# Batch 1's first transform stage partly moved ahead of the main loop, and its frequency groups started at unit 13

## The chip, the cores and the metric

The kernel runs on one core of one Trainium2 chip. The metric is the time of one execution in microseconds of device time (us). The kernel before takes 1475.23 us in the median of three runs (1474.01 to 1475.56). The core has TensorE (PE; its weight loads are shown apart as PEld), VectorE (DVE), ScalarE (ACT), GpSimd (POOL) and SyncE (SP), which here only issues transfers. Each engine works through its own instructions in the order in which the program lists them.

## What is computed

Cut to what matters (the layers follow one another; `relu`, `soft` and the top-1 choice are written out in words):

```
X = rfft(x, axis=1)                       # x: 8 batches, 3072 positions, 256 channels
Y = (Xr w_r - Xi w_i + b_r) + i (Xr w_i + Xi w_r + b_i)
Y = soft(Y, 0.01)                         # real and imaginary part apart
y = irfft(Y, n=3072)                      # 24576 tokens of 256 channels
g = s * relu(y w_in)**2 + b ; z = g w_out # 256 -> 2048 -> 256
e = argmax(z w_gate)                      # one of 8 experts per token
out = gate * (relu(z w1[e]) w2[e])        # for the first 768 tokens of each expert, else 0
```

## The kernel before, in words

**The transform.** A sequence of 3072 is taken as 48 times 64. The first stage (`f1_mm`, L223) multiplies by a 48-point table: one call takes 8 of the 64 residues of one batch, so a batch has 8 calls. A call reads an x tile of 384 KB that `f1_load` (L210) brought in by two transfers, makes four products (matmul, L235; two instructions each in fp32, so 8 in the trace), copies the result out of PSUM (for every batch but 0 with one ACT copy of 128x1024, L239, into a ring `z` of two buffers) and stores it to DRAM with two transfers (L248), for later batches by way of a list `later` that is emptied by `flush` after the next unit. The second stage works on 12 pairs of frequency groups per batch: `g_load` (L255) reads one pair from DRAM across all 64 residues, so it needs the stores of all 8 calls; `g_a` transforms (L269) and copies the result to `l` (ACT L272, DVE L273); `g_b` and `g_b2` multiply by the channel matrices (L346) and add the biases; `g_soft` thresholds; `g_c` is the inverse transform of the pair (L384) and stores it to `vd`. The last stage, `i2_do` (L485), loads eight tiles per batch from `vd` (`i2_load`, L397), multiplies (64 small products, L416), copies (ACT L419) and transposes on DVE (L431).

**The main loop.** What follows the transform is done in units, 64 per batch. `s_unit` (L755) makes 256 of the 2048 hidden columns for 384 tokens (four products, L764), a relu on ACT (L769) and a square on DVE (L770) into a ring `q` of nine buffers (`QB`). Eight units together give cheap logits (L784). All other work is hung on units by hand: `put(at, f, rank)` says before or after which unit a piece is emitted, and within a unit pieces go by rank, then by `at`. A planner `best(lo, hi, work)` chooses the unit of a few pieces by the load noted so far. Since every engine works in program order, this table is the schedule.

**Before the main loop** batch 0 is transformed alone: eight first-stage calls, 36 idle products (`warm`, L440: a product with a tile of zeros, written to a PSUM bank that nothing reads), then `first_groups` (L467), a list of 30 steps in which pairs 0 to 11 of batch 0 go by, with the conversion of the weights `moe_w_in` (blocks `CONV_A`) hung on eleven of these steps. A block's raw words are fetched (`conv_load`, L537), two ACT instructions make its low part and a square (`conv_low`, L559), six DVE instructions join the words (`conv_word`, L571), and `conv_use` splits the result. The fp32 results of `CONV_A` use the same nine buffers `q` as the squares later do, and so does the bias tile `bias0` (L188) for batch 0.

**The second conversion.** The blocks `CONV_B` (eight, of `moe_w_out`) have their raw words in the ring `x` of four buffers that also holds the x tiles of the first stage. One step n of `conv_items` (L623) fetches block n+3, makes the low part and the words of block n+2, transposes block n-1 (L606, ACT copy L608) and makes the gate products of block n-2 (L619). Blocks 0 to 3 are fetched in steps 16 to 22 of `first_groups`; three steps (`CONV_EARLY`) run ahead of `i2_do(0, 0)`, the other nine in units 0 to 6 (`MOE_CONV_AT`). So blocks 4 to 7 are fetched in units 0 to 3. In units 0 to 10 there are also the 32 pieces of `gram_items` (L656; products L665 and L677), and in units 7 to 11 `load_bias` and `bound_items` (L690), which end with the bound weights `wogb` that the first logits, in unit 13, need.

**Batch 1 and 2 in the units of batch 0.** The first-stage calls of batch 1 stand at units 6, 8, ... 20, those of batch 2 from unit 27. Each call of batch 1 also loads the x tile three calls ahead (`x_ahead`, L461); the first three are loaded in unit 4. The pairs of batch 1 begin at unit 26 (`FIRST_GROUPS_AT`) and follow each other every two units; `g_load` runs one to three units ahead of `g_a`. `load_bias1` and `sum_mix`, which `g_b` needs, stand at unit 15. Between `first_groups` and `i2_do(0, 0)` stand 11 idle products.

Of the kernel before, what the change touches and what calls it, by code (L numbers as in the profile page):

```python
# [130 lines left out]
INV_LOAD_AT = 55  # L131
FIRST_GROUPS_AT = 26
GROUP_LEAD = 10
# [13 lines left out]
WARM_F1 = 36  # L147
WARM_GROUPS = 11
MOE_CONV_AT = (0, 1, 2, 3, 3, 4, 5, 6, 6, 7, 7)
# [6 lines left out]
class Kern:  # L156
# [29 lines left out]
    def load_bias0(self):  # L186
        nc, I = self.nc, self.I
        b = self.stage()[:, 0:2 * C]  # L188
        for gi in range(2):
            for k in range(2):  # L190
                src = I[("b_r", "b_i")[(gi + k) % 2]].rearrange("(o c) -> o c", o=1)
                nc.sync.dma_start(out=b[64 * k:64 * k + 64, gi * C:(gi + 1) * C], in_=src.to_broadcast([64, C]))
        self.bias0 = b
# [16 lines left out]
    def f1_load(self, b, c):  # L210

        if b == 0 and c > 3:
            xp = (self.mo.tile([128, 4, C], F32, tag="u", name="x", bufs=3) if c < 7 else
                  self.wk.tile([128, 4, C], F32, tag="z", name="x", bufs=2))
        else:
            xp = self.wk.tile([128, 4, C], F32, tag="x", name="x", bufs=4)
# [6 lines left out]
    def f1_mm(self, b, c):  # L223

        nc = self.nc
        xp = self.xt.pop((b, c))
        if b or c % 2 == 1:
            ph = self.hp.tile([128, 2, 512], F32, tag="h", name="pz")
            ps = [ph[:, 0], ph[:, 1]]
        else:  # L230
            ps = [self.psum("pz") for r in range(2)]
        for k in range(2):
            for r in range(2):
                h = slice(64 * r, 64 * r + M1)
                nc.tensor.matmul(ps[r][64 * k:64 * k + 64, :], self.f1[h], xp[h, 2 * k:2 * k + 2].rearrange("p a c -> p (a c)"),  # L235
                                 start=True, stop=True, skip_group_check=True)
        if b:
            zz = self.wk.tile([128, 4, C], F32, tag="z", name="z", bufs=2)
# [208 lines left out]
    def f1_items(self, b):  # L447
        it = []
        for k in range(8):
            def f(k=k):  # L450
                self.f1_mm(b, k)
                if b:
                    self.x_ahead(8 * b + k + (XP if b < 3 else XP - 1))
            it.append(f)
# [104 lines left out]
    def conv_low(self, k):  # L559
# [3 lines left out]
        raw = self.cv[k]  # L563
        if raw.dtype == F32:
            return
# [1248 lines left out]
    def run(self):  # L1814
# [6 lines left out]
        with ExitStack() as es, tc.manual_schedule():  # L1821
# [54 lines left out]
            for n, k in enumerate((16, 18, 20, 22)):  # L1876
                extra[k] = lambda n=n: self.conv_load(CONV_B[n])
            for k, f in enumerate(gr):
                f()
# [4 lines left out]
                if not conv:  # L1884
                    conv = self.conv_items(CONV_B, 3, 2)
            self.warm(WARM_GROUPS)
            self.i2_load(0, 0)
            self.i2_load(0, 1)
            for k in range(CONV_EARLY):
                conv.pop(0)()  # L1890
            self.i2_do(0, 0)

# [52 lines left out]
            def groups(b):  # L1945
                at, cyc, steps = 64 * (b - 1) - GROUP_LEAD, GROUP_CYCLE, GROUP_STEPS
                if b == 1:
                    at, cyc, steps = FIRST_GROUPS_AT, 2, FIRST_STEPS
                elif b == B - 1:
# [19 lines left out]
            def plan_batch(b):  # L1969
                u = 64 * b  # L1970
                if b == 0:
# [10 lines left out]
                    put(52, lambda: self.route_consts(pp))  # L1982
                    put(15, lambda: (self.load_bias1(), self.sum_mix()))
                    put(54, lambda: (clear(self.list), clear(self.gd)))
                    put(4, lambda: self.x_ahead(7 + XP), 0)
                if b == B - 2:
# [28 lines left out]
                if b == 0:  # L2015
                    for k in range(8):
                        put(6 + 2 * k, self.f1_items(1)[k], 4)
                        put(27 + int(2.9 * k), self.f1_items(2)[k], 4)
                elif b + 2 < B:
# [93 lines left out]
```

## Time and profile before

| | |
|---|---|
| median of 3 runs | 1475.23 us (1474.01 to 1475.56) |
| the profiled execution's own time | 1474.91 us |
| its span, first to last instruction | 1473.1 us |
| PE busy | 1373.8 us, 93% of the span |
| DVE, ACT, POOL busy | 63%, 57%, 7% |
| mean granted clock of TensorE | 0.98 |

An engine's busy time says how long its instructions ran, not whether they ran at full speed: the granted clock of TensorE, a share of its full 2.4 GHz, stands beside it. A matmul row's count is of instructions, and `ph` or `pz` in a row is the tile written. In a timeline the bracket at the end of a row is the idle time of that engine just before it and the instruction that ended it. SPq is SP's queue of transfers. Time zero is the span's start.

### The profile page before, as it was taken

How to read it: one execution, taken by the hardware profiler on the slowest of the kernel's cores; microseconds unless marked ns; L12 is line 12 of the kernel's file. 1: busy time of each engine (PE TensorE's matmuls, PEld its weight loads, DVE VectorE, ACT ScalarE, POOL GpSimd, SP SyncE). 2: the span in 40 equal slices, each digit the busy share in tenths (PEclk: the TensorE clock that was granted, in tenths of full speed). 3: DMA queues.
4: the chain of work that ended last, by engine and by line, in shares of the span. 5: the costliest groups of instructions: out<-in, count | busy, mean ns of one | idle time of the engine just before them, and what ended most of it. 6: DMA issues, size and time to landing. Idle time of an engine off the chain costs nothing.

```text
span 1473.1 us, 32429 instructions
## 1 busy us (share of the span) xinstructions
PE 1373.8 (93%) x12877; PEld 1136.3 (77%) x12877; DVE 922.5 (63%) x2151; ACT 841.3 (57%) x1198; POOL 99.8 (7%) x116
## 2 busy tenths in 40 slices
PE   8997769999999989999999999999999799999995
PEld 5886557788777767787788778877888688988884
DVE  1878336775555887667677667766677666665600
ACT  1436635465555656676676666766656677763321
POOL 0000000000000002102000200200020002122020
PEclk9998989999999999999999999999999999999998
DMA  9736656655554456657755766665555779740080
GB/s 240 252 132 176 159 160 162 170 150 148 160 145 134 110 133 175 164 144 146 197 149 140 182 170 159 147 184 144 132 149 162 231 224 240 223 124 16 12 310 13
DMA packets 275586, 234.51 MB, mean 159 GB/s; under 512 B 121405, under 2 KB 229695, under 8 KB 274912
## 3 DMA queue, kind: packets, MB, share of 16 engines
q1 hardware_dynamic: 269728, 226.34, 56.2%
q0 software_dynamic: 3824, 2.82, 0.8%
q10 hardware_dynamic: 1872, 3.18, 0.6%
q8 instruction: 103, 1.69, 0.5%
q14 instruction: 59, 0.48, 0.1%
HBM read 114.17 MB, written 118.29 MB: 158 GB/s over the span
## 4 chain that ended last, share of the span: by engine, by line
PE 68%; DVE 15%; ACT 6%; DMA 5%; issue 3%; SPq 2%; POOL 0%; ACTq 0%; DVEq 0%; POOLq 0%
PE ph L764 20%; PE pmx L346 14%; PE pi L384 4%; PE pz L235 4%; ACT r L769 3%; PE pf L269 3%; PE phx L981 3%; PE ya L1461 3%; PE pi L416 3%; PE lg L784 2%; DVE qb L770 2%; PE ph L1512 2%; PE po L1522 2%; PE ya L996 2%; PE ph L981 1%
## 5 line engine op out<-in xcount | busy, mean ns | idle before, releaser
L769 ACT ACTIVATE r<-ph 128x768 bf16<-128x768 f32 (+1 forms) x512 | 399.5, 786 | 198.7 <-PE ph L764 167.4
L764 PE MATMUL ph<-ah,win 128*128 128x384 f32 (+1 forms) x2048 | 482.1, 361 | 21.7 <-ACT r L769 18.4
L770 DVE TENSOR_TENSOR qb<-r 128x768 bf16<-128x768 bf16 (+1 forms) x512 | 272.5, 534 | 258.5 <-ACT r L769 254.5
L764 PEld LDWEIGHTS ph<-ah,win 128*128 128x128 f32 x2048 | 342.1, 193 | 106.6 <-ACT r L769 48.1
L346 PE MATMUL pmx<-wm,l 128*128 128x256 f32 x1196 | 293.9, 384 | 5.9 <-DVE l L308 1.4
L346 PEld LDWEIGHTS pmx<-wm,l 128*128 128x128 f32 x1196 | 221.6, 190 | 35.8 <-DVE l L308 3.4
L918 POOL DMA_INDIRECT list<-c,x x64 | 61.3, 957 | 871.6 <-DVE c L914 854.5
L384 PE MATMUL pi<-t,e 128*128 128x256 f32 x384 | 99.3, 381 | 2.4 <-DVE t L341 0.8
L269 PE MATMUL pf<-d,zp 128*128 128x128 f32 x672 | 89.7, 277 | 4.4 <-DMA zp<-zd 4.0
L269 PEld LDWEIGHTS pf<-d,zp 128*128 128x128 f32 x672 | 87.2, 193 | 5.9 <-DMA zp<-zd 5.0
L416 PEld LDWEIGHTS pi<-f1t,u 48*64 48x64 f32 x4096 | 68.7, 136 | 26.4 <-issue 9.7
L239 ACT COPY z<-pz 128x1024 f32<-128x1024 f32 x56 | 56.8, 1014 | 56.2 <-PE pz L235 46.8
L235 PE MATMUL pz<-x,f 48*64 48x512 f32 x512 | 75.1, 657 | 10.9 <-DVE at L431 6.5
L416 PE MATMUL pi<-f1t,u 48*64 48x48 f32 x4096 | 76.2, 224 | 8.7 <-ACT z L239 6.8
L386 ACT COPY v<-pi 128x512 f32<-128x512 f32 x96 | 56.3, 587 | 42.6 <-PE pi L384 39.6
L431 DVE STREAM_TRANSPOSE at<-pi 128x384 f32<-128x384 f32 x128 | 66.9, 560 | 21.2 <-ACT ah L419 18.2
L384 PEld LDWEIGHTS pi<-t,e 128*128 128x128 f32 x384 | 70.2, 189 | 10.6 <-DVE t L341 2.7
L419 ACT CAST ah<-pi 128x768 fp32r<-128x768 f32 x64 | 51.3, 801 | 40.7 <-PE pi L416 40.7
L800 ACT COPY ls<-lg 128x384 f32<-128x384 f32 (+1 forms) x64 | 53.8, 841 | 31.5 <-PE lg L787 28.1
L341 DVE TENSOR_TENSOR t<-t,cl 128x512 f32<-128x512 f32 x96 | 66.5, 693 | 3.3
L272 ACT COPY l<-pf 128x512 f32<-128x512 f32 x84 | 49.2, 586 | 23.3 <-PE pf L269 20.0
L1025 DVE TENSOR_TENSOR xq<-xq 128x512 f32<-128x512 f32 x48 | 33.0, 690 | 39.4 <-ACT xq L1024 39.3
(421 smaller groups left out, 1760.6 us busy)
## 6 DMA issues: line engine op xcount, KB each, us to landing
x<-x SPq DMA_DIRECT2D x128, 192.0 KB
zp<-zd SPq DMA_DIRECT2D x96, 256.0 KB
u<-vd SPq DMA_DIRECT2D x128, 192.0 KB
ad<-at SPq DMA_DIRECT2D x256, 96.0 KB
out<-zero SPq DMA_DIRECT2D x96, 256.0 KB
zd<-z SPq DMA_DIRECT2D x112, 192.0 KB
vd<-v SPq DMA_DIRECT2D x84, 256.0 KB
sd<-xq SPq DMA_DIRECT2D x32, 256.0 KB
```

The costliest lines, as they stand in the source:

```text
L235: nc.tensor.matmul(ps[r][64 * k:64 * k + 64, :], self.f1[h], xp[h, 2 * k:2 * k + 2].rearrange("p a c -> p (a c)"), start=True, stop=True, ...
L269: nc.tensor.matmul(pv[:, h, :, gi * 64:gi * 64 + 64], zp[:, gi, h * 128:(h + 1) * 128], self.d[:, 2 * p + gi, :].rearrange("p (t m) -> p t ...
L341: nc.vector.tensor_tensor(out=t, in0=t, in1=cl, op=ALU.subtract)
L346: self.nc.tensor.matmul(o, part(h), w[:, h], start=start and h == 0, stop=stop and h == 1, skip_group_check=True)
L384: nc.tensor.matmul(ps[:, gi * C:(gi + 1) * C], self.e[:, 2 * p + gi], t[:, gi * C:(gi + 1) * C], start=True, stop=True)
L416: nc.tensor.matmul(o[64 * k:64 * k + 64, :, n], u[p, n, 128 * k + h:128 * k + 128:2], self.f1t[p], start=True, stop=True, skip_group_check ...
L431: nc.vector.transpose(out=at[:, :, :, h], in_=pv[:, M1 * h:M1 * (h + 1)])
L764: nc.tensor.matmul(ps[:, j, :n], self.win[:, k, f], ah[:, k, t0:], start=(k == 0), stop=(k == 1))
L769: nc.scalar.activation(out=r, in_=ps[:, :, :n], func=AF.Relu)
L770: nc.vector.tensor_tensor(out=q, in0=r, in1=r, op=ALU.mult)
L918: self.nc.gpsimd.indirect_dma_start(out=self.lists[n], out_offset=bass.IndirectOffsetOnAxis(ap=x[:, n:n + 1], axis=0), in_=c[:, n:n + 1], ...
L981: nc.tensor.matmul(ps[:, j], w[:, c, f], x[:, c], start=(c == 0 and k == 0), stop=(c == 1 and k == 2))
```

## The change

- Tiles 0 to 3 (`SPLIT`) of batch 1's x are loaded during `first_groups` (steps 21, 23, 24, 25), each as two tiles in the ring `q` with four transfers instead of two. Their first-stage calls copy PSUM back into the same tiles with two ACT copies of 128x512, and store with four transfers. Even calls among them take PSUM banks of the ring `bg` instead of `h`.
- Calls 0 to 2 of batch 1 run between `first_groups` and `i2_do(0, 0)`, in turn with the three early conversion steps; call 3 in unit 1, calls 4 to 7 in units 5, 6, 7, 8. The idle products there go from 11 to 5.
- Blocks 4, 5, 6 of `CONV_B` are fetched in that same place, and the low part of block 0 is made in step 26 of `first_groups`.
- The other x tiles of batch 1 are loaded in units 2, 3, 4, 4, the first three of batch 2 in unit 18; calls of batch 1 load nothing ahead any more. `bias0` moves from the ring `q` to a tile `kw2`.
- The pairs of batch 1 begin at unit 13 and follow every three units; `load_bias1` and `sum_mix` move to unit 11. The calls of batch 2 stand at units 20, 23, 27, ... 46.

```diff
-FIRST_GROUPS_AT = 26
+FIRST_GROUPS_AT = 13
+SPLIT = 4
-WARM_GROUPS = 11
+WARM_GROUPS = 5
@@ load_bias0
-        b = self.stage()[:, 0:2 * C]
+        b = self.wk.tile([128, 2 * C], F32, tag="kw2", name="bias0", bufs=1)
@@ f1_load
+        if b == 1 and c < SPLIT:
+            xp = self.xt[b, c] = [self.mo.tile([128, 2, C], F32, tag="q", name="x", bufs=QB) for k in range(2)]
+            xv = self.I["x"][b].rearrange("(a n) c -> a n c", n=M2)
+            for k in range(2):
+                for r in range(2):
+                    n2 = 8 * c + 4 * k + 2 * r
+                    self.nc.sync.dma_start(out=xp[k][64 * r:64 * r + M1], in_=xv[:, n2:n2 + 2])
+            return
@@ f1_mm
-        if b or c % 2 == 1:
+        split = b == 1 and c < SPLIT
+        if (b and not split) or c % 2 == 1:
...
+        if split:
+            for r in range(2):
+                nc.scalar.copy(out=xp[r].rearrange("p a c -> p (a c)"), in_=ps[r])
+
+            def put():
+                for r in range(2):
+                    for k in range(2):
+                        n2 = 8 * c + 4 * k + 2 * r
+                        nc.sync.dma_start(out=self.zs[b][n2:n2 + 2].rearrange("n q c -> q n c"), in_=xp[r][64 * k:64 * k + M1])
+            self.later.append(put)
+            return
@@ f1_items
-                if b:
+                if b > 1:
                     self.x_ahead(8 * b + k + (XP if b < 3 else XP - 1))
@@ conv_low
-        if raw.dtype == F32:
+        if raw.dtype == F32 or k in self.cw:
             return
@@ run
+            for c, k in enumerate((21, 23, 24, 25)):
+                extra[k] = lambda c=c: self.x_ahead(8 + c)
+            extra[26] = lambda: self.conv_low(CONV_B[0])
...
-            self.warm(WARM_GROUPS)
             self.i2_load(0, 0)
             self.i2_load(0, 1)
+            f1b = self.f1_items(1)
             for k in range(CONV_EARLY):
+                f1b[k]()
                 conv.pop(0)()
+                if k < 2:
+                    self.conv_load(CONV_B[4 + k])
+                self.flush()
+            self.conv_load(CONV_B[6])
+            self.warm(WARM_GROUPS)
             self.i2_do(0, 0)
...
-                    at, cyc, steps = FIRST_GROUPS_AT, 2, FIRST_STEPS
+                    at, cyc, steps = FIRST_GROUPS_AT, 3, FIRST_STEPS
...
-                    put(15, lambda: (self.load_bias1(), self.sum_mix()))
+                    put(11, lambda: (self.load_bias1(), self.sum_mix()))
...
-                    put(4, lambda: self.x_ahead(7 + XP), 0)
+                    for k, n in enumerate((2, 3, 4, 4)):
+                        put(n, lambda k=k: self.x_ahead(12 + k), 0)
+                    put(18, lambda: self.x_ahead(15 + XP), 0)
...
-                        put(6 + 2 * k, self.f1_items(1)[k], 4)
-                        put(27 + int(2.9 * k), self.f1_items(2)[k], 4)
+                        if k >= CONV_EARLY:
+                            put((1, 5, 6, 7, 8)[k - 3], f1b[k], 4)
+                        put(20 + int(3.8 * k), self.f1_items(2)[k], 4)
```

## Rows read from the trace of the kernel before

**Rows 1.** The page: busy tenths of PE and granted clock in 40 slices
```profile
PE   8997769999999989999999999999999799999995
...
PEclk9998989999999999999999999999999999999998
```

**Rows 2.** Busy time by stretch: length, PE, PEld, DVE, ACT, POOL, granted clock, DMA share, GB/s
```profile
105.00:117.00 12.00, 8.53 (x95) 6.83 (x96) 9.45 (x17) 6.01 (x10) 0.00 (x0) 0.98 0.49 132
117.00:169.00 52.00, 40.83 (x440) 32.92 (x440) 32.61 (x79) 33.18 (x59) 0.00 (x0) 0.91 0.65 185
...
186.00:209.00 23.00, 11.51 (x119) 9.40 (x116) 4.70 (x12) 6.64 (x11) 0.00 (x0) 0.70 0.72 195
209.00:345.00 136.00, 133.38 (x1241) 108.81 (x1241) 89.31 (x209) 70.10 (x110) 3.82 (x8) 1.00 0.57 150
```

**Rows 3.** Timeline of PE, units 14 to 26 of batch 0
```profile
174.99 1.11 PE L416 MATMUL pi<-f1t,u 48*64 48x48 f32 x64
...
193.80 1.96 PE L416 MATMUL pi<-f1t,u 48*64 48x48 f32 x64 [6.77 <-ACT z L239]
...
197.60 3.98 PE L764 MATMUL ph<-ah,win 128*128 128x256 f32 x16 [0.69 <-ACT r L769]
...
205.62 2.07 PE L269 MATMUL pf<-d,zp 128*128 128x128 f32 x8 [4.04 <-DMA zp<-zd]
```

**Rows 4.** The chain that ended last, 183 to 206 us: start, us, what
```profile
184.85 7.82 DMA zd<-z
...
194.15 2.52 DMA zd<-z
...
200.76 4.82 DMA zp<-zd
```

**Rows 5.** Timeline of PE from the idle products to unit 8
```profile
107.59 4.91 PE L445 MATMUL warm<-zero 128*128 128x256 f32 x22
113.75 0.33 PE L416 MATMUL pi<-f1t,u 48*64 48x48 f32 x4 [1.25 <-DMA u<-vd]
...
130.77 0.65 PE L619 MATMUL pg<-wt,wg 128*32 128x64 f32 x16 [4.31 <-ACT wt L608]
...
159.08 1.09 PE L235 MATMUL pz<-x,f 48*64 48x512 f32 x8
```

**Rows 6.** Timeline of DVE, words of `CONV_B`: each block begins or goes on here
```profile
109.48 0.69 DVE L585 SCALAR_TENSOR_TENSOR ct<-cm,ct 128x512 f32<-128x512 f32 x1 [1.92 <-ACT cm L567]
...
121.03 0.41 DVE L580 TENSOR_SCALAR ct<-cr 128x512 int32<-128x512 int32 x1
...
128.95 0.43 DVE L580 TENSOR_SCALAR ct<-cr 128x512 int32<-128x512 int32 x1 [3.50 <-DMA cr<-moe_w_out]
...
137.60 0.38 DVE L580 TENSOR_SCALAR ct<-cr 128x512 int32<-128x512 int32 x1
```

**Rows 7.** The chain that ended last, 98 to 214 us
```profile
123.84 5.08 DMA cr<-moe_w_out
...
171.21 1.05 PE lg L784 x12
```

**Rows 8.** Waits of SP's queue, 60 to 105 us: total, times, longest
```profile
SPq L400 <- DMA vd<-v: 23.4, 1, 23.4
```

**Rows 9.** Timeline of SP's queue: start, time over all issues
```profile
110.55 1.79 SPq L400 DMA_DIRECT2D u<-vd  x4
```

**Rows 10.** Timeline of all engines around one pair of batch 1
```profile
223.47 0.72 PE L764 MATMUL ph<-ah,win 128*128 128x256 f32 x4
...
223.75 0.59 ACT L272 COPY l<-pf 128x512 f32<-128x512 f32 x1 [0.42 <-PE pf L269]
```

**Rows 11.** All transfers that write or read x tiles
```profile
DMA to landing us min/median/max: 2.6/4.1/5.7
```

**Rows 12.** Busy time by stretch, columns as in rows 2
```profile
140.00:145.00 5.00, 4.63 (x107) 3.92 (x105) 4.61 (x9) 3.23 (x6) 0.00 (x0) 1.00 0.45 125
8.00:12.00 4.00, 4.00 (x24) 1.58 (x22) 1.38 (x2) 1.17 (x2) 0.00 (x0) 1.00 1.07 230
```

More of the change, by code (lines that the diff above doesn't have):

```diff
@@ L234, in f1_mm @@
                 h = slice(64 * r, 64 * r + M1)
-                nc.tensor.matmul(ps[r][64 * k:64 * k + 64, :], self.f1[h], xp[h, 2 * k:2 * k + 2].rearrange("p a c -> p (a c)"),
+                rhs = xp[k][h] if split else xp[h, 2 * k:2 * k + 2]
+                nc.tensor.matmul(ps[r][64 * k:64 * k + 64, :], self.f1[h], rhs.rearrange("p a c -> p (a c)"),
                                  start=True, stop=True, skip_group_check=True)
+        if split:
[8 more added lines that the diff above has]
+            return
         if b:
```

## The prediction

> **What bounds the kernel now.** I began with the page. TensorE reads 9 tenths or more busy in 33 of 40 slices, and its clock eight tenths or more in all of them [rows 1]. So the general limit is TensorE's own work, and only places where it idles or runs at the lower clock can give time back. The weak place away from the ends is the fourth to sixth slice of 37 us, where PE reads 7, 7 and 6 [rows 1]. The busy times by stretch place it: from 117 to 169 us PE is busy 40.83 of 52 us, from 186 to 209 only 11.51 of 23 us at a granted clock of 0.70, and from 209 on 133.38 of 136 us at 1.00 [rows 2]. From 209 on nothing is to be had but work removed; the change removes almost none. So I looked at what ends each wait of PE between 105 and 209 us.
>
> In the timeline of PE the large ones are 6.77 us before an inverse product (a `z` copy on ACT was late), 0.69 and 4.04 us before the first `g_a` of batch 1 (its `zp` was late) [rows 3], 4.31 us in the second conversion, and 1.25 us for `u` after the idle products [rows 5]. The chain says why. A first-stage store took 7.82 us to land, the last one 2.52, and the pair's load 4.82 [rows 4]: with the calls of batch 1 in units 6 to 20 and nothing else for PE, the trip to DRAM and back is bare. The 4.31 us are the fetch of raw block 4, which took 5.08 us from its issue at 123.84 [rows 7]; DVE too waited 3.50 us for it [rows 6].
>
> **The change, part by part.** Times are against the profiled execution's own 1474.9 us (span 1473.1); the median of the runs is 0.3 us higher.
>
> *(a) Three calls in place of idle products: -3.2 us.* A call occupies PE for about 1.06 us (1.09 less the overlap with its follower) [rows 5]. Calls 0 to 2 leave units 6 to 10 and stand where 11 idle products took 4.91 us, 0.45 each. Three calls and 5 products are 5.4 us, so `i2_do(0, 0)`, which waited for `u` anyway [rows 5], starts at the same time. The six products removed are worth nothing by themselves: the wait for `u` would take their place. The cover of the early loads is SP's own idleness: it waits 23.4 us, once, for the last `vd` store [rows 8], and the 16 transfers for four tiles, at 0.45 us of SP each (four in 1.79 us [rows 9]) 7.2 us, fit in that. The six ACT copies, each like the copy of 0.59 us of the same shape [rows 10], lie in ACT's idle half of the stretch 105 to 117 (6.01 of 12 busy [rows 2]). If SP or ACT were late, `i2_do` would slip; I bound that by 0 and +2. The extra eight stores go out behind the `u` loads, so they delay no one before unit 0.
>
> *(b) The wait for raw block 4 goes: -6.9.* Blocks 4 to 6 are now fetched as soon as blocks 0 to 2 are joined, well before unit 1. That is 4.31 us of idle time [rows 5] and the low clock after it. An inverse stage takes 1.96 us at the low clock and 1.11 at full [rows 3], a factor of 1.77; some 6 us ran so after 130.77, which is 2.6 us lost.
>
> *(c) A new wait for raw block 7: +6.0.* This is the price of the reordered ring `x`. Its buffers now go raw 0 to 6, x tile 4 (unit 2), x tile 5 (unit 3), raw 7. So raw 7 takes the buffer of raw 5 and SP cannot issue it before DVE has joined block 5. DVE goes from block to block in 4.3 us (two blocks from 128.95 to 137.60 [rows 6]). Its 1.92 us wait for ACT's `cm` falls away, since the low part of block 0 is made earlier, so block 3 begins at about 119.1 instead of 121.03 [rows 6], block 4 at 123.5, and block 5 is joined at about 132. With 4 to 5.08 us for the transfer [rows 7] raw 7 is there at 136 to 137.5. But block 7's low part stands in the same unit 3 on ACT, ahead of the copies that the transposes and the gram products of units 3 and 4 need. PE resumed at 130.77 in unit 2 before [rows 5]; without that wait and with call 3 in unit 1 it gets about two units further, to the transpose of block 5 in unit 4, by some 134.8 (an estimate from these rows), and ACT, after two instructions for the low part and one copy, is free near 138.2: 3.4 us idle, and the low clock after it once more, 2.6 us. The ends are 0 (PE arrives later than I think) and +10 (PE stops earlier in unit 3). So the conversion gives almost nothing: one late fetch is traded for another.
>
> *(d) The bare trip of the z tiles goes: -16.0.* The calls 4 to 7 stand in units 5 to 8, each about 4 us long because the gram products and the conversion are there, so a `z` buffer has two such units to be stored. The idle 6.77, 0.69 and 4.04 are 11.5 us [rows 3]. The work from 193.8 to 209 was some 10.3 us of busy time at about half clock; at full it is 10.3 / 1.77 = 5.8, which makes 4.5 us more.
>
> *(e) The same trip at the new place: +2.0.* Unit 8 was at 157 to 160 us (its call at 159.08 [rows 5]); with two more calls ahead of it call 7 ends near 162, its copy of 1 us and its store (2.52 us to land, two issues [rows 4, 9]) are done near 167, and 2.5 to 4.82 us [rows 4] later `zp` is there: 170 to 172. `g_a` in unit 13 is reached at about 169. Yet the first logits, in the same unit, wait for `wogb` until 171.21 now [rows 7], and that chain is as long as before, so most of the wait is one that PE has already. `load_bias1` and `sum_mix` at unit 11 queue behind it on SP and DVE and can hold `g_b` of pair 0 another microsecond. Ends: 0 and +6.
>
> *(f) Pairs every three units: +2.5.* Between `g_a` and `g_b` there is now often only one unit's product, 0.72 us less the overlap with its follower, so some 0.57 [rows 10], while before a `g_c` stood there too. The copy of `l` begins 0.28 us after that product starts and takes 0.59 [rows 10], so about 0.3 us is bare. For eight of the twelve pairs, those without a first-stage call or an inverse stage between, that is 2.5 us. Ends: 0 and +6. In return the units 26 to 53 hold less; they were nearly full already (133.38 of 136 [rows 2]), so nothing is gained there.
>
> *(g) The x tile for batch 2's first call*, loaded at unit 18 and used at unit 20, some 5 us later: x tiles land in 2.6 to 5.7 us [rows 11], behind five other issues on SP: +0.5 (0 to +2). *(h) An inverse stage moves*: with load noted from unit 13 on, the planner puts the third one into unit 12 instead of 14, into the wait for `wogb`: -1.0 (0 to -1.1).
>
> The sum is -3.2 - 6.9 + 6.0 - 16.0 + 2.0 + 2.5 + 0.5 - 1.0 = -16.1. So 1474.9 becomes 1458.8 and the median about **1459.0 us**. What follows unit 64 is hung on units and PE-bound, so it moves forward as a block.
>
> **The clock.** Fewer idle products and a stretch of transposes could leave TensorE at the lower of its two levels (1.2 and 2.4 GHz). The rows speak against it: first-stage products alone held 1.00 from 8 to 12 us, and 140 to 145 us, full of transposes, ran at 1.00 [rows 12]. The Trainium skill, page "TensorE: Matmul & The Clock Gate", section "Part 4: PE-mode transpose", says that products in transpose mode do not count as activity in the same way and do not bring the full clock. By that rule the units 0 to 9 would run at the lower level; this trace does not bear it out for these transposes.
>
> **The rivals.**
>
> 1. *Half of it is given back* (1464.5 to 1472): raw 7 at its upper end (+10 instead of +6), `zp` at +6 and the pairs' latency at +6 make 11.5 us less gain, 1470.5. For it: three new dependences in a row, each with little slack. Against: `wogb` and the conversion's DVE work cover them in part.
> 2. *More* (1447 to 1454): PE never reaches the transpose before ACT is free, (c) is 0, and 1453 follows. For it: DVE and ACT are near their limit in 130 to 145 us.
> 3. *The change doesn't do what it says*: the early x tiles come late because ring `q` is released by the conversion of `moe_w_in`, and PE waits where it idled before. Then (a) is lost: 1462. Against: SP's 23.4 us of waiting [rows 8].
> 4. *About the same*: `zp` late for three or four pairs. One late pair cost 4.04 us and about 1.0 of low clock [rows 3]; three give 15 us back, 1474. It decides from the point where a pair's load takes longer than the three units, about 8 us, that it runs ahead. The longest trip seen, 7.82 [rows 4], is just under.
> 5. *Slower*: the clock does not come back in units 0 to 12, since the work there is transposes and small products. From 117 to 169 us PE is busy 40.83 us at 0.91 [rows 2], some 37 us at full speed; at the low level 37 x 1.77 = 65.5, so 24.7 us more: 1483.7. It decides if the clock is still low in unit 5. The rule of the Trainium skill told above would end here.
>
> **How the numbers follow.** Chances: forecast (1454 to 1464.5) 0.59, rival 1 0.20, rival 2 0.09, rival 3 0.05, rival 4 0.04, rival 5 0.03. A measurement of this kernel tells about 0.2%, 3 us, from no change. Faster: 0.59 + 0.20 + 0.09 + 0.05 = 0.93; same 0.04; slower 0.03. The range leaves out rivals 4 and 5, the far end of rival 1 and that of rival 2: 1449 to 1468.
>
> **What would show it.** Right: no wait of PE over 3 us on `z` or `zp` between units 9 and 27, `i2_do(0, 0)` still at about 114 us, PE near full with the clock at 1.00 from unit 14 on, an ACT wait of some 4 us for `cr` in unit 3. Wrong: a start of `i2_do` later than 117; a wait for `cr` beyond 6 us or none; repeated waits for `zp` after pair 0; PE under 95% between units 15 and 50; a gain or loss after unit 64.

## The result and the profile after

The changed kernel takes 1465.17 us in the median of 15 runs (1460.98 to 1470.38), the kernel before beside it 1476.64 (15 runs, 1473.53 to 1486.78): a ratio of 0.9917, 95% interval 0.9903 to 0.9932, and 11.5 us between the medians, where 16.1 were forecast. The profiled execution took 1464.19 us with a span of 1462.4, 10.7 less than before.

The page of the changed kernel, busy tenths of PE and its granted clock, which answers to [rows 1]:

```profile
PE   8998799999999989999999999999999799999995
...
PEclk9997999999999999999999999999999999999998
```

The weak place is shorter: the sixth slice went from 6 to 9. But the fourth slice (110 to 146 us) now has a 7 in the clock. Busy time by stretch, columns as in [rows 2]; the first four rows are the changed kernel in the stretches of [rows 2], the last two again the changed kernel, from the start of the relu of unit 0 to that of unit 14, and on to unit 64:

```profile
105.00:117.00 12.00, 9.04 (x106) 5.33 (x105) 10.72 (x20) 8.80 (x16) 0.00 (x0) 0.97 0.61 156
117.00:169.00 52.00, 43.88 (x430) 34.38 (x430) 29.20 (x66) 30.64 (x54) 0.00 (x0) 0.81 0.65 186
186.00:209.00 23.00, 22.57 (x209) 17.15 (x208) 16.16 (x37) 10.79 (x18) 0.65 (x2) 1.00 0.61 140
209.00:345.00 136.00, 131.59 (x1323) 108.04 (x1325) 88.14 (x202) 76.83 (x119) 3.55 (x8) 1.00 0.62 162
...
118.40:179.60 61.20, 49.48 (x542) 38.82 (x540) 34.79 (x89) 38.01 (x68) 0.00 (x0) 0.85 0.60 168
179.60:301.30 121.70, 115.85 (x1118) 92.93 (x1119) 79.98 (x197) 63.47 (x103) 4.20 (x10) 0.99 0.67 165
```

The same two stretches of units in the kernel before:

```profile
118.00:173.70 55.70, 43.06 (x466) 34.25 (x469) 34.14 (x88) 35.49 (x63) 0.00 (x0) 0.90 0.67 187
173.70:315.50 141.80, 126.31 (x1223) 99.45 (x1224) 81.74 (x200) 69.51 (x110) 4.48 (x10) 0.95 0.61 158
```

Cutting by units compares like with like. Each unit has one relu on ACT; the table gives the time between the starts of these relus (us).

| units | before | after | difference | the prediction's steps put there |
|---|---|---|---|---|
| 0 to 14 | 55.6 | 61.2 | +5.6 | +2.3 |
| 14 to 64 | 141.8 | 121.7 | -20.1 | -18.4 |
| 64 to 140 | 234.2 | 233.9 | -0.3 | 0 |
| 140 to 180 | 87.3 | 91.1 | +3.8 | 0 |
| 180 to 511 | 679.3 | 679.3 | 0.0 | 0 |

The last column sorts the steps by units. Units 0 to 14 lose calls 0 to 2 (-3.2, step (a)) and get calls 4 to 7 from units 14 to 20 (four of 1.06, +4.2), an inverse stage and the first `g_a` come in too (+1.1 each), and (b) and (c) lie there (-6.9 + 6.0): +2.3. The rest, -18.4, is in units 14 to 64. The sorting is rough: steps (e) and (h) lie on either side of unit 14, and with both of them ahead of it the column would read +3.3 and -19.4. So at unit 64 the change has gained 14.5 of 16.1 us, too little ahead of unit 14 and somewhat more than forecast behind it, and then it loses 3.8 near unit 158, where nothing was forecast. One profile of each kernel is a rough measure ahead of unit 14: three profiles of the changed kernel's code there (its own, and two of the experiments below) took 61.2, 61.6 and 64.3 us, two of the code before 55.6 and 58.2.

The timeline of PE of the changed kernel, from the first inverse stage to pair 0 of batch 1, which answers to [rows 3, 5]:

```profile
113.97 0.32 PE L438 MATMUL pi<-f1t,u 48*64 48x48 f32 x4 [0.73 <-DMA u<-vd]
...
135.72 0.43 PE L641 MATMUL pg<-wt,wg 128*32 128x64 f32 x16 [1.78 <-DVE wog L643]
...
142.39 0.43 PE L641 MATMUL pg<-wt,wg 128*32 128x64 f32 x16 [1.94 <-ACT wt L630]
...
166.45 1.09 PE L246 MATMUL pz<-x,f 48*64 48x512 f32 x8
...
175.77 1.06 PE L291 MATMUL pf<-d,zp 128*128 128x128 f32 x8
...
177.14 0.62 PE L806 MATMUL lg<-qb,wogb 128*32 128x256 bf16 x16 [0.31 <-DVE wogb L773]
...
180.61 3.36 PE L368 MATMUL pmx<-wm,l 128*128 128x256 f32 x8 [2.08 <-DVE l L299]
```

The waits of 6.77, 4.04 and 4.31 us are gone. `i2_do(0, 0)` starts at 113.97, as before. New are 1.78 us for `wog`, a product of DVE in the conversion, and 1.94 for `wt`, a copy that ACT makes late because of raw block 7. ACT's timeline and that of SP's queue show this wait:

```profile
140.64 0.68 ACT L589 ACTIVATE cm<-cr 128x512 f32<-128x512 f32 x1 [5.33 <-DMA cr<-moe_w_out]
```

```profile
134.89 0.39 SPq L578 DMA_DIRECT2D cr<-moe_w_out  x1
```

SP issues block 7 at 134.89, and ACT stands still for 5.33 us until it is there. What SP does just ahead of that issue, and DVE's last read of raw block 5, whose buffer block 7 takes:

```profile
129.68 2.71 SPq L256 DMA_DIRECT2D zd<-x  x4
132.48 0.87 SPq L229 DMA_DIRECT2D x<-x  x2
133.40 0.43 SPq L625 DMA_DIRECT2D wd<-cf  x1
133.93 0.85 SPq L229 DMA_DIRECT2D x<-x  x2
```

```profile
131.60 0.69 DVE L604 SCALAR_TENSOR_TENSOR ct<-cr,ct 128x512 int32<-128x512 int32 x1
```

The buffer is free at 132.29, and SP shows no wait for DVE after that. The other 2.6 us are SP's own order: it first issues the stores of call 3, after waiting 2.4 us for their copy on ACT, and the x tiles 4 and 5. Last, the place near unit 158: rows of ACT, then PE, then POOL in the changed kernel.

```profile
578.19 0.84 ACT L444 ACTIVATE asq<-ah 128x768 bf16<-128x768 f32 x1
581.66 0.59 ACT L294 COPY l<-pf 128x512 f32<-128x512 f32 x1 [2.63 <-PE pz L246]
```

```profile
583.01 1.00 PE L786 MATMUL ph<-ah,win 128*128 128x384 f32 x4 [1.82 <-ACT r L791]
583.81 3.57 PE L368 MATMUL pmx<-wm,l 128*128 128x256 f32 x8
```

```profile
580.25 1.03 POOL L940 DMA_INDIRECT list<-c,x  x1 [0.30 <-issue]
```

ACT waits 2.63 us ahead of a copy whose input PE had finished near 578.3 (the row names a later product, which the copy does not read). PE then waits 1.82 us for ACT, and its next products run at the lower clock (3.57 us for eight). The last of POOL's eight indirect transfers ends at 580.25 + 1.03 = 581.28, 0.4 us before ACT goes on. In the kernel before the same copy had no wait.

### The profile page after: what moved, and what is told of

The parts are those of the page before. It is cut to its first block, busy times and chain, and to the rows that moved or that the text cites. A ratio compares the mean times of both kernels' runs of the same rounds, so it can differ in the third digit from the quotient of the medians.

```text
span 1462.4 us, 32413 instructions
## 1 busy us (share of the span) xinstructions
PE 1371.0 (94%) x12865; PEld 1133.7 (78%) x12865; DVE 923.9 (63%) x2151; ACT 841.1 (58%) x1202; POOL 99.9 (7%) x116
## 3 DMA queue, kind: packets, MB, share of 16 engines
q8 instruction: 103, 1.69, 0.5%
## 4 chain that ended last, share of the span: by engine, by line
PE 70%; DVE 13%; ACT 6%; DMA 5%; issue 3%; SPq 2%; POOL 0%; ACTq 0%; DVEq 0%; POOLq 0%
PE ph L786 20%; PE pmx L368 14%; PE pz L246 5%; PE pi L406 4%; PE pf L291 3%; ACT r L791 3%; PE pi L438 3%; PE phx L1003 3%; PE ya L1483 3%; PE lg L806 2%; DVE qb L792 2%; PE ph L1534 2%; PE po L1544 2%; DMA zp<-zd 2%; PE ya L1018 2%
## 5 line engine op out<-in xcount | busy, mean ns | idle before, releaser
L786 PE MATMUL ph<-ah,win 128*128 128x384 f32 (+1 forms) x2048 | 480.3, 360 | 20.5 <-ACT r L791 18.8
L368 PE MATMUL pmx<-wm,l 128*128 128x256 f32 x1196 | 297.9, 387 | 9.4 <-DVE l L299 2.8
L261 ACT COPY z<-pz 128x1024 f32<-128x1024 f32 x52 | 52.8, 1015 | 46.1 <-PE pz L246 45.9
```

The costliest lines, as they stand in the source:

```text
L368: self.nc.tensor.matmul(o, part(h), w[:, h], start=start and h == 0, stop=stop and h == 1, skip_group_check=True)
L786: nc.tensor.matmul(ps[:, j, :n], self.win[:, k, f], ah[:, k, t0:], start=(k == 0), stop=(k == 1))
```

## The experiments

Three chips were used. On each, four kernels ran with the kernel before beside them. On the first and the third the kernel before took 66 and 76 us more than above, so times are compared by their ratio to the kernel before on that chip (1542.55, 1479.90 and 1552.46 us), and profiles by stretches of units. Units 64 to 140 take 232.9 to 234.5 us in all of them; the extra time comes later. The stretches (us), the first four kernels from the first chip, the next four from the second, the last four from the third:

| kernel | ratio, 95% interval | units 0 to 14 | 14 to 64 | 140 to 180 |
|---|---|---|---|---|
| raw 7 early | 0.9895 (0.9861 to 0.9929) | 55.4 | 121.8 | 105.9 |
| 11 groups of idle products | 0.9906 (0.9872 to 0.9941) | 59.9 | 121.4 | 106.0 |
| pairs at unit 26 | 1.0014 (0.9982 to 1.0045) | 61.1 | 140.6 | 107.0 |
| before, blocks 4 to 6 early | 0.9984 (0.9955 to 1.0013) | 53.7 | 141.4 | 105.8 |
| changed kernel again | 0.9933 (0.9916 to 0.9949) | 61.6 | 121.0 | 94.1 |
| sum_mix early | 0.9928 (0.9912 to 0.9943) | 63.4 | 119.0 | 94.2 |
| raw 7 and sum_mix early | 0.9911 (0.9892 to 0.9930) | 59.9 | 118.4 | 94.5 |
| pairs every two units | 0.9941 (0.9923 to 0.9960) | 60.7 | 123.0 | 93.7 |
| list later | 0.9847 (0.9801 to 0.9893) | 64.3 | 121.7 | 104.5 |
| before, 12 ACT copies more | 1.0004 (0.9977 to 1.0030) | 58.2 | 141.7 | 105.0 |
| raw 7 early and list later | 0.9831 (0.9789 to 0.9872) | 57.0 | 121.0 | 104.9 |
| raw 7 early again | 0.9835 (0.9788 to 0.9882) | 57.0 | 121.6 | 107.8 |

**The calls moved, the pairs left at unit 26.**

```diff
-FIRST_GROUPS_AT = 13
+FIRST_GROUPS_AT = 26
-at, cyc, steps = FIRST_GROUPS_AT, 3, FIRST_STEPS
+at, cyc, steps = FIRST_GROUPS_AT, 2, FIRST_STEPS
```

> The changed kernel with the pairs of batch 1 at unit 26 and every two units again, all else as changed. Theory: moving the calls covers the trip from z to zp by itself (PE waits under 1 us for zp), but the units 13 to 26 are then empty of pairs and each waits for ACT's relu, some 0.3 to 0.5 us a unit; the time is 3 to 7 us over the changed kernel (1468 to 1472) and still under the kernel before. Rival: the early pairs are what gained; then all of it goes and the time is that of the kernel before (1475 to 1478). Second rival: the start of the pairs is worth nothing, 1464 to 1467.

Ratio 1.0014: nothing is gained, so the rival holds and the theory does not. Waits of PE in this kernel's timeline:

```profile
179.46 0.85 PE L806 MATMUL lg<-qb,wogb 128*32 128x256 bf16 x16 [3.91 <-DVE wogb L773]
...
193.18 2.84 PE L246 MATMUL pz<-x,f 48*64 48x512 f32 x8 [2.92 <-DMA x<-x]
...
213.37 2.08 PE L291 MATMUL pf<-d,zp 128*128 128x128 f32 x8 [6.14 <-DMA zp<-zd]
```

With the calls gone and no pairs there, PE has too little to do in units 13 to 26, and the waits for a transfer are bare as before, only for others. From unit 0 to 64 it takes 61.1 + 140.6 = 201.7 us, 4.3 more than before. The pairs at unit 13 make it 182.9, 18.8 less. So step (d) is one gain of both moves together; the calls alone would not have brought it. (The edit also sets the pairs two units apart again; by the experiment on that below, this is worth 2 us at most.)

**Only blocks 4 to 6 early, in the kernel before.**

```diff
                 conv.pop(0)()
+                if k < 2:
+                    self.conv_load(CONV_B[4 + k])
+            self.conv_load(CONV_B[6])
```

> The kernel before with one part of the change alone: raw blocks 4, 5 and 6 of moe_w_out fetched ahead of the main loop, nothing else moved. Theory (term b): the 4.3 us wait of PE in unit 2 and the low clock after it go, 4 to 7 us less than the kernel before (1470 to 1473). Rival: the wait only moves on, to DVE's words or ACT, and the time stays within 2 us of the kernel before (1475 to 1478).

Ratio 0.9984, no difference that can be told: the rival holds. The wait of 4.31 us [rows 5] is gone, and PE's timeline of this kernel shows what was late next:

```profile
135.68 0.43 PE L619 MATMUL pg<-wt,wg 128*32 128x64 f32 x16 [2.19 <-DVE wog L621]
```

Units 0 to 14 take 1.9 us less than before and by unit 64 2.3 us are gained, where (b) had 6.9. Against the other profile of the code before (58.2 us, with 12 ACT copies from unit 34 on) it is 4.5.

**Raw block 7 ahead of the x tiles**, run twice.

```diff
                     for k, n in enumerate((2, 3, 4, 4)):
                         put(n, lambda k=k: self.x_ahead(12 + k), 0)
+                    put(1, lambda: self.conv_load(CONV_B[7]), 0)
```

> The changed kernel with raw block 7 fetched at unit 1 into the buffer of block 3, ahead of batch 1's x tile 4. Theory: the wait for raw 7 is a real cost of the new ring order, ACT stood 5.3 us and PE 1.9 us after it with the clock low for 3.4 us more, so ACT's wait goes, unit 4 starts about 3 us earlier and the time falls by 3 to 5 us against the changed kernel (1460 to 1462). Rival: DVE's chain of words holds PE there anyway (it waited 1.8 us for a gate transpose on DVE), and the time stays within 1.5 us of the changed kernel.

> Only raw block 7 at the front of unit 1's pieces, once more, beside kernels with the list moved. Theory: 5 us faster than the changed kernel ahead of unit 14, the stall near unit 158 unchanged: 0.988 to 0.989, and 4 to 6 us behind the kernel that also moves the list. Rival: the first profile's 5 us were the accident of a shorter stretch at the lower clock after the first inverse stage (3.4 us in place of 10.2); then ACT's wait for raw 7 still goes, and the gain is 2 to 3 us.

In the first profile ACT's wait, 5.33 us in the changed kernel, is 1.17, and PE has no wait for `wt` in unit 4:

```profile
135.28 0.70 ACT L589 ACTIVATE cm<-cr 128x512 f32<-128x512 f32 x1 [1.17 <-DMA cr<-moe_w_out]
```

```profile
134.53 0.43 PE L641 MATMUL pg<-wt,wg 128*32 128x64 f32 x16 [1.79 <-DVE wog L643]
```

Units 0 to 14 take 55.4 and 57.0 us against 61.2 and 61.6 in the two profiles of the changed kernel. In all four the rest to unit 64 takes 121 to 122 us, so what is gained here is kept: 4 to 6 us is the price of the late fetch, as step (c) had it. The lower figure is the safer one, for a reason that the windows of 10.4 us from unit 0 on show. The first row is the changed kernel, the second raw 7 early (first run), the third the kernel before with only blocks 4 to 6 early, whose code to there is that of the kernel before, the fourth the kernel before:

```profile
116.00:126.40 10.40, 8.55 (x61) 7.53 (x54) 7.55 (x15) 6.90 (x12) 0.00 (x0) 0.51 0.96 293
```

```profile
117.80:128.20 10.40, 9.14 (x72) 7.68 (x73) 9.04 (x19) 7.51 (x15) 0.00 (x0) 0.84 0.98 288
```

```profile
115.60:126.00 10.40, 8.57 (x89) 8.01 (x80) 9.42 (x17) 5.69 (x10) 0.00 (x0) 0.51 0.82 227
```

```profile
116.00:126.40 10.40, 8.47 (x68) 7.79 (x68) 8.84 (x18) 5.73 (x10) 0.00 (x0) 0.84 0.44 89
```

The granted clock is 0.51 or 0.84 there, with the change and without it. The second run of raw 7 early had the lower one too (0.50) and is still 4.2 us shorter than the changed kernel: PE is idle for 9.3 us instead of 11.7, and its products take 47.7 instead of 49.5. Two more pairs, each on one chip, differ only in raw 7: the two kernels with `sum_mix` early and the two with the list later. Their stretch to unit 14 shrinks by 3.6 and 7.3 us, and counted from the start of the execution unit 14 begins 4.4 and 4.5 us earlier (180.6 against 185.0, 180.9 against 185.4). In time over the whole program the medians of these pairs differ by 4.0 and 6.1 us, inside the intervals; against the changed kernel itself no run on one chip shows it.

The runs do not tell two causes of the late fetch apart, the buffer and SP's order, since the edit changes both.

**More idle products.**

```diff
-WARM_GROUPS = 5
+WARM_GROUPS = 11
```

> The changed kernel with the 11 idle products back in place of 5. Theory: the low clock from 116 to 126 us comes from the waits of PE around the first inverse stage, which no idle product ahead of them covers; the clock falls at the same place, and 2.7 us of products more delay the first inverse stage by 1 to 2 us, since the wait for u there is only 1.5 us; the time is 0 to 3 us longer than the changed kernel (1465 to 1468). Rival: six products fewer let the clock fall for longer; then it is back at full by 121 us as in the kernel before, and the time falls by 2 to 4 us (1461 to 1463).

Units 0 to 14 take 59.9 us, 1.3 less than in the changed kernel. But unit 0 starts at 121.20, 2.0 us later than in raw 7 early on the same chip (119.20), whose code to there differs only by these products: what they may give behind the first inverse stage they take ahead of it, as the theory had it. The clock from 117.0 to 127.4 us was 1.00 in this profile, but the waits in units 3 and 4 stay, and the products themselves take 5.02 us instead of 2.43. The ratio, 0.9906, cannot be told from the changed kernel's. One profile does not show whether the products or the accident seen above made the clock stay.

**The changed kernel again**, without an edit.

> The changed kernel itself once more, as the measure for the three kernels beside it: about 0.991 of the kernel before. Its profile is to tell two readings of the loss ahead of unit 14 apart. If the long stretch at the lower clock that follows the first inverse stage (10.2 us in the changed kernel's first profile, 3.4 us in the kernel with raw 7 early, and 10.2 us in the kernel that only fetches blocks 4 to 6 early, whose code to there is that of the kernel before with its 3.4) is an accident of the execution, it may be 3.4 here, and unit 14 then starts about 3 us earlier. If the change brings it, it is 10.2 again. The idle 2.6 us of ACT and the 3.4 us of lower clock near 580 us should be absent if they too are accidents; the profile's gain at unit 64 is 14 us or more and is then kept to the end.

The lower clock after unit 0 is there once more. So is the loss at unit 158, and it is larger: 94.1 us for units 140 to 180 against 87.3. It is no accident, then: all four kernels of the second chip, which all have the change, lose 6.4 to 7.2 us there. ACT's row of this run:

```profile
583.02 0.59 ACT L294 COPY l<-pf 128x512 f32<-128x512 f32 x1 [4.53 <-remote]
```

**`load_bias1` and `sum_mix` earlier, alone and with raw 7.**

```diff
-                    put(11, lambda: (self.load_bias1(), self.sum_mix()))
+                    put(9, self.load_bias1, 0)
+                    put(7, self.sum_mix, 6)
```

> load_bias1 goes from unit 11 to the front of unit 9 and sum_mix from unit 11 to the end of unit 7. Theory: the 2.08 us that PE waits before g_b of pair 0 for the DVE copy into l come from DVE working off sum_mix and the bound chain ahead of that copy; two instructions of 0.69 us fewer in that queue take 1.4 us off the wait, and the 3.4 us of lower clock near 181 us may go with it (1.5 us more): 1 to 3 us faster than the changed kernel, seen by unit 22. Rival: the copy waits for the bound chain itself and for ACT, not for sum_mix; the wait stays at 2.0 and the time within 1 us.

> Raw block 7 fetched at the front of unit 1's pieces, ahead of the x tiles, together with load_bias1 and sum_mix earlier. Theory: the two waits are separate, so the gains add: 5 us ahead of unit 14 (as the profile with raw 7 early showed against the changed kernel) and 1 to 3 after it; 6 to 8 us faster than the changed kernel, about 0.987 of the kernel before. Rival: what is gained ahead of unit 14 only makes PE arrive earlier at the first logits and at g_b of pair 0, which wait for the same DVE chain; then it is 3 us or less.

In the first of these PE's 2.08 us for `l` are gone, but it waits elsewhere in the same pair:

```profile
180.27 1.81 PE L291 MATMUL pf<-d,zp 128*128 128x128 f32 x8 [0.90 <-DMA zp<-zd]
...
185.61 1.97 PE L368 MATMUL pmx<-wm,l 128*128 128x256 f32 x8 [1.33 <-ACT r L791]
```

0.90 and 1.33 make 2.23: `zp` and a relu were next in line. To unit 64 it takes 182.4 us, the changed kernel beside it 182.7. The rival holds in its result, though not by its reason. With raw 7 early as well it is 178.3 us, 4.4 less, which is about what raw 7 gave alone. The median is 1466.24 us against 1468.83, 2.6 us less: the theory's 6 to 8 are not there, and the rival's 3 or less fits, inside the intervals.

**Pairs every two units**, from unit 13.

```diff
-at, cyc, steps = FIRST_GROUPS_AT, 3, FIRST_STEPS
+at, cyc, steps = FIRST_GROUPS_AT, 2, FIRST_STEPS
```

> The changed kernel with the pairs of batch 1 every two units again, still from unit 13. Theory (the step on pairs every three units): a g_c stands between g_a and g_b again and covers the copy of l, so the 0.2 to 0.3 us per pair go, 1 to 2.5 us faster. Rival: PE is full in these units either way, the pairs are only packed closer while calls of batch 2 and inverse stages share the units, and a pair's trip from DRAM (about 4 us behind other issues) has two units instead of three: waits for zp come back and it is 0 to 6 us slower than the changed kernel.

Units 14 to 64 take 123.0 us against 121.0. PE waits 1.23 us for a `zp`, 1.69 for a relu ahead of `g_b` and up to 1.03 for DVE ahead of first-stage calls. The rival holds in this profile, with 1.3 to 2.0 us against the two of the changed kernel; the ratios, 0.9941 and 0.9933, cannot be told apart.

**The list of batch 1 four units later, alone and with raw 7 early.**

```diff
-return [a, c, d, e] + GAP * (b < self.B - 1) + [f] + ...
+return [a, c, d, e] + GAP * ((b < self.B - 1) + 4 * (b == 1)) + [f] + ...
```

> The eight indirect transfers that POOL sends to the list of batch 1 (in units 156 to 160) go four units later. Theory: the 3.6 to 6.6 us that the changed kernel loses near unit 158 are instruction words of ACT that arrive late: their transfers land only when POOL's eight transfers end (at 581.3 us, the same moment), and ACT stands still until then. With POOL's transfers later, ACT's words land in time, the wait before the copy into l in unit 159 is gone, and what is gained at unit 64 is kept to the end: 4 to 6 us faster than the changed kernel, about 0.989 of the kernel before. Rival: the stall belongs to the place in ACT's program and comes wherever the list is; then it is still there at unit 158 and the time is within 1 us.

> Raw block 7 fetched at the front of unit 1's pieces and the list of batch 1 four units later. Theory: the gains add, 5 us ahead of unit 14 and 4 to 6 us near unit 158: about 0.985 of the kernel before, the fastest so far. Rival: either part is worth nothing by itself, 0.989 or more.

The edit moves the eight transfers and the small step that works out their positions. Two kernels of one chip that differ only in this can be compared: raw 7 early (units 156 to 160 take 18.4 us), and the same with the list later (9.5 us, as in the kernel before). ACT's row and PE's rows in the first, then DVE's and POOL's in the second:

```profile
597.07 0.80 ACT L441 CAST ah<-pi 128x768 fp32r<-128x768 f32 x1 [8.56 <-PE pi L438]
```

```profile
588.45 0.80 PE L438 MATMUL pi<-f1t,u 48*64 48x48 f32 x34
590.40 0.28 PE L438 MATMUL pi<-f1t,u 48*64 48x48 f32 x3 [1.15 <-issue]
...
596.14 0.89 PE L438 MATMUL pi<-f1t,u 48*64 48x48 f32 x20 [0.28 <-issue]
```

```profile
604.02 0.56 DVE L792 TENSOR_TENSOR qb<-r 128x768 bf16<-128x768 bf16 x1 [6.21 <-issue]
```

```profile
593.75 0.98 POOL L940 DMA_INDIRECT list<-c,x  x1 [43.85 <-DVE c L936]
...
602.65 0.92 POOL L940 DMA_INDIRECT list<-c,x  x1 [0.30 <-issue]
```

On this chip it is not ACT that stands still in unit 158 but TensorE. The 64 products of an inverse stage, 1.18 us in the changed kernel's profile, come in small groups from 588.45 to 597.03, and ACT waits for them. With the list later this is gone from unit 158. But another stall comes where the list now is: DVE stands still until 604.02, with POOL's last transfer ending at 603.57, and units 160 to 168 take 24.0 us instead of 17.5. Of 8.9 us 6.5 are given back. So it is shown that the stall goes with POOL's eight transfers, against the rival. That moving them saves 4 to 6 us is not borne out: 2.4 us stay in these units, and the medians of the two kernels are 1523.07 and 1522.72. The list alone at the later place did the same (9.5 and 23.9 us). On a chip where ACT is the one that stands still, as in the changed kernel's profile, the list was not moved.

**Is ACT's longer program the cause?** The kernel before, with twelve small copies on ACT.

```diff
+        self.idle = pp.tile([128, 1], F32, tag="idle", name="idle")
...
+                    for k in range(12):
+                        put(34 + 2 * k, lambda: nc.scalar.copy(out=self.idle, in_=self.ident[:, 0:1]))
```

> The kernel before, with twelve copies of 128x1 on ACT that nobody reads, one each in units 34, 36 to 56. ACT is 57% busy, so the copies themselves should cost under 1 us. Theory: the kernel before escapes the stall only because ACT's program is there some eight instructions shorter than the changed kernel's, so that it runs out of words a little later than POOL's transfers end; with twelve more it stands still in unit 158 too, 3.6 to 6.6 us slower than the kernel before (1.003 to 1.0045). Rival: the stall has to do with what else the change moved; then there is none, and the time is the same within 1.5 us.

Ratio 1.0004. This says nothing for or against. ACT waits 8.54 us there, but for TensorE, whose inverse stage takes 8.56 us as in raw 7 early. The kernel before with only its blocks early, on the first chip, shows the same without any extra copies (8.29 us). So on these two chips the stall is there without the change and is no loss by it, and the question of ACT's program stays open: it needs a chip on which the kernel before runs through.

## Why the prediction was right, and where it was off

The mechanism held: the bare trip of the z tiles is gone, PE is full from 186 us on (22.57 of 23 us to 209 at 1.00, against [rows 2]), and the median lies in the range. It is 6 us above the forecast, though, at the near edge of the times of rival 1 (1464.5 to 1472), and what was given back is not what that rival named. The range holds because it takes in most of that rival. By the steps:

(a) Right: `i2_do(0, 0)` at 113.97, 0.73 and 0.75 us of waiting for `u`. Neither SP nor ACT was late.

(b) This step failed. It charged the whole wait and the low clock after it, and did not name what was late next, which was DVE's `wog` at 1.8 to 2.2 us in every kernel with the blocks early. Alone it gave 1.9 to 2.3 us, not 6.9. That run had the clock of 0.51 after unit 0, which cost 1.6 us between the two runs of raw 7 early (57.0 against 55.4); with that added it is under 4, and against the other profile of the code before it is 4.5.

(c) Right in place and nearly in size (4 to 6 us by its removal, 6.0 forecast), but only half in its cause, so the size is in part luck. DVE's last read of raw block 5 ended at 132.29, about when the forecast had the block joined (132). SP issued block 7 at 134.89, because the stores of call 3 and two x tiles stood ahead of it in its queue, which the step left out. The transfer then took 5.66 us (DVE reads block 7 from 140.58 on), and ACT waited 5.33 us where 3.4 were forecast. PE came later than forecast as well: it ended the product ahead of its wait at 140.45, not 134.8, and idled for 1.94 us.

By the runs (b) is worth 2 to 4.5 us instead of 6.9, and (c) costs 4 to 6 instead of 6.0. Together that is up to 5 us less than forecast; the stretch to unit 14 shows 3.3 less, or 2.3 with (e) and (h) counted there.

(d) Right, and larger than its sum: units 14 to 64 gained 20.1 with all other steps, 18.4 forecast. The step credits the gain to the earlier calls; with these alone nothing was gained, and it took the earlier pairs too. PE's idle time there fell from 141.8 - 126.3 = 15.5 to 5.9 us, and the clock rose from 0.95 to 0.99.

(e) Right in size by another cause, which is luck. The wait of 2.08 us is for a copy by DVE, not for `zp`; when DVE was relieved, `zp` and a relu took its place.

(f) The waits are the forecast's, about 0.2 us per pair where they show, but going back to two units gains nothing (1.3 to 2.0 us more in one profile). So the distance of three is no price by itself.

(g), (h) No wait for an x tile shows at unit 20, and the inverse stage ran ahead of the first logits. Nothing to correct.

The other step that failed is the sentence that what follows unit 64 moves forward as a block; a gain or loss after unit 64 was one of the signs named for a wrong prediction. It does so to unit 156. Then ACT stands still, at a place that the change does not touch, and 3.8 us are lost in the first profile and 6.8 in the second, against the one profile of the kernel before. In sum -16.1 + 3.3 - 1.7 + 3.8 = -10.7, the difference of the spans (0.3 us less in units 64 to 140 and 0.3 more ahead of unit 0 cancel).

The rivals: 4 needs a late `zp`, and so does 1 in part; the longest wait for one is 1.19 us. 3 falls with (a). 2 had its place right, since taking the raw-7 wait away does bring 4 to 6 us. 5 was half there: the clock from 117 to 169 us is 0.81. But it comes back among the transposes, as the window after the first one shows:

```profile
126.40:136.70 10.30, 8.52 (x105) 6.60 (x106) 9.21 (x19) 7.42 (x15) 0.00 (x0) 1.00 0.76 216
```

By the rule of the Trainium skill, page "TensorE: Matmul & The Clock Gate", section "Part 4: PE-mode transpose", transposes do not bring the full clock. This stretch, with transposes in every unit, is at 1.00, but it does not decide on that rule: of PE's 8.52 us only 3.9 are transposes (`pwg` and `pwt`), the rest are other products. The same holds for the stretch from 140 to 145 us that the prediction set against the rule [rows 12], with 2.3 of 4.63 us.

## What to carry to other kernels

When a stall is removed, look for the next instruction of the same engine that is late for another reason, and charge only the time to there; a fetch made early in the kernel before, by itself, was worth a third to two thirds of what was charged for it here. A transfer that waits for a buffer also waits for all that stands ahead of it in its queue, so ask when the queue gets to it. Two moves that fill the same gap (calls away, other work in) are to be costed as one. And a block of work that "only moves" can still lose time where another engine's transfers sit, so compare a trace by units over its whole length, not only at the edit.

## What was not expected of the hardware

**The clock after unit 0.** The same code was granted 0.51 or 0.84 over the 10.4 us after the first inverse stage, from one execution to the next, and the difference is worth some 1.6 us between the two runs of raw 7 early. A single profile can't be read more finely than that there.

**Engines that stand still while POOL sends its list.** While POOL works through eight indirect transfers, one every 1.2 us, another engine comes to a stop, or nearly so. On the chip of the result and on the second it is ACT, for 2.6 to 4.8 us. On the first and the third it is TensorE in the middle of an inverse stage, which takes 8.2 to 8.6 us there in place of 1.18; with the list later, DVE stands still for 5.5 and 6.2. The rows of the engine that stops name no cause (`issue`, `remote`) or an instruction that it does not depend on. The DMA rows suggest one. From 566 to 581.1 us the trace of the changed kernel has no packet of the two instruction queues; in the microsecond after it, when POOL's last transfer has just been sent, there is one of each:

```profile
q8 instruction: 1, 0.02, 6.0%
...
q14 instruction: 1, 0.01, 1.9%
```

In the kernel before the two come at the same point (595.2 to 596.2 us, the same two rows), and ACT had copies to make until 594.33 and then waited for a product. In the four profiles of the second chip both packets come 0.6 to 1.3 us after the last transfer, and ACT goes on 0.9 to 2.1 us after them. That instruction words held up are what stops ACT fits this, but no run here isolates it. It does not fit every case: with the list later, a packet of q14 comes among POOL's transfers (at 600.04), and DVE still stands until 604.02. Why the kernel before escapes on its chip stayed open. The Trainium skill, page "Runtime: NRT & Kernel Launch", section "Instruction fetch mechanics", has the fetch of the next block mostly hidden behind the execution of the current one. If the words are the cause, the rows here do not agree beside such transfers. On the first and the third chip the stalls are longer and come with more of the lists. In the second run of raw 7 early ACT waited 10.04 us beside the first list (POOL busy from 540.96), over 7 of them for TensorE's inverse stage, and 6.40 beside the third, of which two rows of ACT and POOL:

```profile
697.71 0.81 ACT L822 COPY ls<-lg 128x384 f32<-128x384 f32 x1 [6.40 <-remote]
```

```profile
696.54 0.92 POOL L940 DMA_INDIRECT list<-c,x  x1 [0.31 <-issue]
```

ACT goes on 0.25 us after POOL has sent its last one (696.54 + 0.92 = 697.46).
